# A Fourier mixing block with its feed-forward block: the first batch's first products, and the order of the weight rounding ahead of step 0

## The chip, the core and the metric

The kernel runs on one core of a Trainium2 chip. TensorE (PE) multiplies, VectorE (DVE), ScalarE (ACT) and GpSimd (POOL) do elementwise work, and SyncE (SP) and ACT issue the transfers. The metric is the device time of one execution in microseconds, lower being better. The kernel before takes 1934.93 us, the median of three runs (1934.9 to 1937.18).

## The reference

```
X = np.fft.fft(x, axis=1); X = np.fft.fft(X, axis=2)      # x: 8 x 3008 x 256
x = X.real.reshape(24064, 256)
h = x @ w_in                                              # 256 x 2048
g = h * (1 / (1 + exp(-1.702 * h)))
out = g @ w_out                                           # 2048 x 256
```

For each of the 8 batches a two-dimensional Fourier transform is taken along the sequence (3008 rows) and the model axis (256), its real part goes through a feed-forward block with the quick GELU. The weights arrive as 64-bit floats and are rounded to 32 bits on the core.

## The kernel before

The sequence length is split as 47 x 64. The *first products* (`mix_first` for batch 0, `mix1` for the others) combine the 47 rows that share a residue jj with a cosine or sine table; their result is written to DRAM (`Td`, the *spill*) and read back in another order (`t4`, the *fill*). `rotate` corrects one column, `stage2` multiplies by the 64-point tables and DVE transposes the result into `pq`. The transform along the model axis is not done on the data: it is folded into `w_in` (`fold_w`, chunk by chunk, into `wcs`). After that come 384 *steps*, 8 batches x 3 blocks x 2 halves x 8 pairs of feature blocks. Step t runs `hidden` (four 128x128 products into `pa` and `pb`), `rows` (DVE makes the four arguments of the GELU from `pa`, `pb`, the row `nb` and the per-feature column `af2`), `activate` (the GELU on ACT) and, three steps later, `product` (seven or eight products with `wo` and `wt` into four accumulators).

Every engine works through its instructions in the order in which the code calls them, so the order of the calls is the schedule. Around the change it is this.

- `load_first` (line 225) brings x of batch 0 in sixteen transfers, half of them on SP's queue and half on POOL's: 128 partitions, as two halves of 64, the even and the odd part of the 64 residues; some rows are loaded twice. `tab1` (0.8 MB, first-product tables) comes on ACT's queue.
- `fold_first(g)` (line 232) adds and subtracts x and its mirror for eight groups of four slots: two DVE additions of 128x508 and one POOL copy of 128x8 per group, in the order 0, 7, 1, 6, 2, 5, 3, 4.
- `mix_first(k)` (line 239), four calls, makes 32 products each on 64x64 pieces of the array; four pieces can run beside each other. Between its two phases ACT copies two columns (line 248) as a join. `spill` and `fill(0, 0, 4)` follow.
- A chunk of weights goes through `bounds` (POOL clamps into `m`, line 360; DVE or ACT squares into `g`; ACT makes the low part `r` in two passes), `rounded` (three DVE passes of 128x1024, lines 373 to 376) and `finish` (one or two POOL additions, line 380). There are four chunks of `w_in` ("in") and four of `w_out` ("out"). A chunk of `w_in` then passes `fold_w` (four products of 128x512, line 418, and two ACT copies into `wcs`). `fold_w` ends with a row that ACT doubles and a small transfer that lays it out as four columns of `af2` (line 425).
- Before step 0, chunk in 0 is rounded and folded; in 1 is rounded after `stage2`; out 0, in 2, out 1, in 3, out 2 and out 3 are rounded inside steps 0 to 6 (`ahead`, line 632), one per step, and chunks 1, 2, 3 of `w_in` are folded in steps 1, 3 and 5 (`early`, line 638). Chunk n serves steps 2n and 2n+1 of each group of eight.
- `warm(n)` issues products on a constant tile whose result nobody reads.

Of the kernel before, what the change touches and what calls it, by code (L numbers as in the profile page):

```python
# [36 lines left out]
NM = 48  # L37
# [23 lines left out]
def tables(S, D):  # L61
# [13 lines left out]
    up = np.zeros_like(w1[:, :NJ + 1])  # L75
    up[:, 1:NJ, :, 0], up[:, 1:NJ, :, 1] = cos[:, :NJ:-1], -sin[:, :NJ:-1]
    up[:, e0, :, 1], up[:, o0, :, 1] = cos[:, NJ], sin[:, NJ]
    w0 = np.zeros((2, 64, NJ + 1, NG * NU, 2))
    for half, w in enumerate((w1[:, :NJ + 1], up)):
        w0[half, :32], w0[half, 64 - (NA - 32):] = w[:32], w[32:]  # L80
    sign = np.repeat([1.0, -1.0], 64)

    c, q = np.divmod(np.arange(NJ), 16)
    j, k2 = (4 * (q // 2) + 2 * (q % 2) + c)[:, None], np.arange(NB)[None, :]
    beta = 2.0 * np.pi * ((j * k2) % NB) / NB
    m2 = np.zeros((NU, 2, NJ, 2, NB))
    rot = np.zeros((NU, 2, NJ, NU, 2, NJ))
    ends = np.stack([np.ones(NB), 1.0 - 2.0 * (np.arange(NB) % 2)])
    for i in range(NU):
        m2[i, 0, :, 0], m2[i, 1, :, 0] = np.cos(beta), -np.sin(beta)  # L90
        m2[i, 0, :, 1], m2[i, 1, :, 1] = np.sin(beta), np.cos(beta)
        m2[i, :, 0, 0] = m2[i, :, 0, 1] = ends
        for n in range(NJ):
            rot[i, 0, n, i, 1, n], rot[i, 1, n, i, 0, n] = (1.0, -1.0) if n else (0.0, 0.0)
        rot[i, 0, 0, i, 0, 0] = rot[i, 1, 0, i, 1, 0] = 1.0
# [6 lines left out]
    small = [t.reshape(128, -1) for t in (m2, rot, cd)]  # L102
    pad = 64 - NM
    w1 = np.pad(w1.reshape(NA, -1), ((0, 128 - NA), (0, pad)))
    w0 = np.concatenate([w0.reshape(128, -1), np.zeros((128, pad)), sign[:, None]], 1)
# [4 lines left out]
def kernel(ctx: ExitStack, tc, x, w_in, w_out, tab1, tab2, out):  # L110
# [24 lines left out]
    small = const.tile([128, 2 * NB + 128 + 4 * H], F32, tag="small", name="small")  # L135
    m2 = small[:, 0:2 * NB].rearrange("p (c n) -> p c n", c=2)
    rot = small[:, 2 * NB:2 * NB + 128]
    cd = small[:, 2 * NB + 128:].rearrange("p (i c d) -> p i c d", i=2, c=2)
    wcs = [const.tile([128, DF], F32, tag=f"wcs{i}", name=f"wcs{i}") for i in range(2)]

    wo = const.tile([128, NF // 2, 4, H], F32, tag="wo", name="wo")
    wt = const.tile([128, NF // 2, 4, H], F32, tag="wt", name="wt")
    af2 = const.tile([128, NF], F32, tag="af2", name="af2")
    ones = const.tile([1, 128], F32, tag="ones", name="ones")

# [76 lines left out]

    room = {}

    def load_first(lo, hi):
        for g in range(2):
            for half, eng in enumerate((nc.sync, nc.gpsimd)):
                p = 64 * half + 32 * g
                eng.dma_start(out=xt[p:p + 32, lo:hi, :].rearrange("p j d -> p (j d)"),  # L229
                              in_=view(x, (NB * (NA - 32) * g + NJ * half + lo) * D, [NB * D, 32], [1, (hi - lo) * D]))  # L230

    def fold_first(g):

        t, e = xt[:, 4 * g:4 * g + 4, :], room[g]
# [4 lines left out]
    def mix_first(k):  # L239


        ks = k, 7 - k
        ps = [bank("ps1") for _ in ks]
        for phase in range(2):
            if phase:

                for n in range(2):
                    nc.scalar.copy(af2[:, n:n + 1], ps[n][:, D + n * (H + 1):D + n * (H + 1) + 1])
            for at in range(4)[::-1 if phase else 1]:
                r, even = divmod(at, 2)  # L250
                for half in (phase, 1 - phase):
                    n = half ^ phase
                    for c in range(2):
                        jj = 4 * ks[n] + 2 * r + c
                        c0, c1 = (0, H + 1) if even ^ half ^ phase else (H + 1, D)
                        slot, first = ((NB - jj) % NJ if half else jj), c0 == 0
# [9 lines left out]
    def placed(k):  # L266
        return 2 * k if k < 4 else 16 + 2 * k
# [449 lines left out]
```

## Time and profile before

| | us |
|---|---|
| median of three runs | 1934.93 |
| the profiled execution, its own time | 1932.74 |
| its span on the core | 1930.7 |
| PE busy | 1902.4 (99%) |
| DVE, POOL, ACT busy | 1406.3, 765.0, 673.9 |
| step 0's first product starts | 43.86 |
| first product of step 8 (second half of block 0) starts | 95.92 |

The span is counted from the first to the last instruction of the core; the profiled execution's own time is 2.04 us longer. A line of the timeline gives the start and the length of a run of equal instructions, the engine, the source line, the operation, what it writes and reads, how many there were, and in brackets how long the engine stood idle before it and what ended that. Matmuls of 32-bit floats appear as two records each.

### The profile page before, as it was taken

What the parts mean: (1) busy time and instruction counts of PE and PEld (TensorE: products, weight loads), DVE (VectorE), ACT (ScalarE), POOL (GpSimd) and SP (SyncE); (2) the same over time, 40 slices, a digit from 0 to 9 for tenths busy, and PEclk for the clock granted to TensorE, in tenths of its full rate; (3) what the DMA queues carried; (4) which work ended last, traced back from release to release, by engine and by line L of the source; (5) the groups of instructions that cost most, each with busy time, mean ns of one, the idle gap of its engine ahead of it and who ended that gap; (6) DMA issues with size and microseconds to landing.
All of it is one profiled execution on the core that took longest, in us unless ns stands there. A gap on an engine that the chain in (4) does not pass through costs nothing.

```text
span 1930.7 us, 29514 instructions
## 1 busy us (share of the span) xinstructions
PE 1902.4 (99%) x10822; PEld 1666.2 (86%) x10822; DVE 1406.3 (73%) x2924; ACT 673.9 (35%) x928; POOL 765.0 (40%) x1061
## 2 busy tenths in 40 slices
PE   7899999999999999999999999999999999999998
PEld 4698888988889888888889888898888988889887
DVE  4777777876777767877777677776777777777766
ACT  4633333333333333333333333333333333333332
POOL 3665323542245322552235523364323642223222
PEclk8999999999999999999999999999999999999999
DMA  8720550227203452126322262221820223202201
GB/s 282 178 51 10 110 65 12 51 55 112 17 12 59 67 92 17 25 45 107 51 28 48 40 102 38 18 49 43 121 20 13 18 48 56 17 12 27 17 12 22
DMA packets 145552, 104.54 MB, mean 54 GB/s; under 512 B 105474, under 2 KB 128290, under 8 KB 143712
## 3 DMA queue, kind: packets, MB, share of 16 engines
q1 hardware_dynamic: 142976, 99.07, 30.4%
q0 software_dynamic: 384, 2.10, 0.4%
q8 instruction: 86, 1.41, 0.3%
q10 hardware_dynamic: 2048, 1.48, 0.3%
q14 instruction: 58, 0.48, 0.1%
HBM read 59.36 MB, written 48.01 MB: 56 GB/s over the span
## 4 chain that ended last, share of the span: by engine, by line
PE 96%; DMA 2%; POOL 1%; issue 1%; DVE 0%; ACT 0%; SPq 0%; ACTq 0%; POOLq 0%; DVEq 0%
PE po L515 59%; PE pa L448 17%; PE pb L448 17%; PE ps L210 1%; PE ps L314 1%; DMA xt<-in_x_dram 1%; DMA raw<-in_moe_w_in_dram 1%; DMA Td<-xt 0%; POOL wo L380 0%; PE ps L214 0%; POOL xt L229 0%; PE psw L418 0%; PE ps L259 0%; DVE e L237 0%; POOL wst L380 0%
## 5 line engine op out<-in xcount | busy, mean ns | idle before, releaser
L489 POOL TENSOR_TENSOR s<-h 128x256 f32<-128x256 f32 (+1 forms) x376 | 270.7, 720 | 1091.8 <-ACT h L477 1026.1
L515 PE MATMUL po<-s,wt 128*128 128x256 f32 (+1 forms) x2256 | 599.7, 375 | 0.0
L452 ACT COPY v<-pa 128x512 f32<-128x512 f32 (+1 forms) x384 | 222.2, 579 | 1063.6 <-PE pa L448 1063.6
L462 DVE TENSOR_TENSOR h<-v,pb 128x512 f32<-128x512 f32 (+1 forms) x384 | 259.2, 675 | 405.9 <-PE pb L448 399.5
L515 PEld LDWEIGHTS po<-s,wt 128*128 128x128 f32 x2256 | 428.6, 190 | 48.3
L515 PE MATMUL po<-h,wo 128*128 128x256 f32 (+1 forms) x1632 | 469.7, 375 | 0.1
L477 ACT ACTIVATE h<-h 128x1024 f32<-128x1024 f32 (+1 forms) x384 | 401.0, 1044 | 17.0 <-DVE h L472 14.0
L448 PE MATMUL pa<-pq,wcs 128*128 128x256 f32 (+1 forms) x1536 | 393.9, 379 | 2.9 <-ACT wcs L420 1.6
L448 PE MATMUL pb<-pq,wcs 128*128 128x256 f32 (+1 forms) x1536 | 387.9, 375 | 2.5 <-DVE dif L465 2.3
L515 PEld LDWEIGHTS po<-h,wo 128*128 128x128 f32 x1632 | 310.0, 190 | 36.0 <-issue 0.5
L448 PEld LDWEIGHTS pa<-pq,wcs 128*128 128x128 f32 x1536 | 286.7, 190 | 51.7 <-issue 11.2
L465 DVE SCALAR_TENSOR_TENSOR dif<-nb,af,pb 128x256 f32<-128x256 f32 (+1 forms) x768 | 328.5, 470 | 1.6 <-DMA af<-row 1.6
L448 PEld LDWEIGHTS pb<-pq,wcs 128*128 128x128 f32 x1536 | 291.5, 190 | 36.6 <-DVE dif L465 2.7
L490 POOL TENSOR_TENSOR s<-h 128x256 f32<-128x256 f32 (+1 forms) x376 | 276.7, 736 | 0.0
L472 DVE TENSOR_TENSOR h<-pa,dif 128x512 f32<-128x512 f32 (+1 forms) x448 | 265.5, 605 | 13.2
L515 PE MATMUL po<-h,wt 128*128 128x256 f32 (+1 forms) x752 | 220.3, 375 | 0.0
L515 PE MATMUL po<-s,wo 128*128 128x256 f32 (+1 forms) x752 | 220.3, 375 | 0.0
L493 DVE TENSOR_TENSOR s<-h,s 128x256 f32<-128x256 f32 (+1 forms) x376 | 202.2, 538 | 12.9
L492 DVE TENSOR_TENSOR s<-s,h 128x256 f32<-128x256 f32 (+1 forms) x376 | 178.0, 473 | 4.3 <-POOL s L489 4.3
L515 PEld LDWEIGHTS po<-s,wo 128*128 128x128 f32 x752 | 142.9, 190 | 16.1
L515 PEld LDWEIGHTS po<-h,wt 128*128 128x128 f32 x752 | 142.9, 190 | 16.1
L196 POOL TENSOR_TENSOR xt<-xt 111x510 f32<-111x510 f32 x56 | 74.1, 1323 | 4.4
(67 smaller groups left out, 697.2 us busy)
## 6 DMA issues: line engine op xcount, KB each, us to landing
out_dram<-os SPq DMA_DIRECT2D x284, 64.0 KB
Td<-xt SPq DMA_DIRECT2D x14, 768.0 KB
t<-Td SPq DMA_DIRECT2D x7, 1536.0 KB
xt<-in_x_dram SPq DMA_DIRECT2D x14, 512.0 KB
xt<-Xr SPq DMA_DIRECT2D x14, 512.0 KB
nb<-pq SPq DMA_DIRECT2D x23, 256.0 KB
out_dram<-os SPq DMA_DIRECT2D x96, 56.0 KB
Xr<-in_x_dram SPq DMA_DIRECT2D x7, 752.0 KB
```

What stands on the lines that cost most here:

```text
L196: eng.tensor_tensor(low, low, free(t, up + D - 1, [-D, 2], [-1, D - 1]), op=ALU.add)
L448: nc.tensor.matmul(ps[:, i * 256:i * 256 + n], lhsT=wcs[cs][:, f * 128:(f + 1) * 128], rhs=pq[:, cs, ks], start=True, stop=True)
L452: nc.scalar.copy(two(v[:], n), two(pa[:], n))
L462: nc.vector.tensor_tensor(two(h[:], n), two(v[:], n), two(pb[:], n), op=ALU.add)
L465: nc.vector.scalar_tensor_tensor(dif[:, i * 256:i * 256 + n], nb[:, ks], af2[:, f:f + 1], pb[:, i * 256:i * 256 + n], op0=ALU.mult, op1=AL ...
L472: nc.vector.tensor_tensor(free(h[:], 512 + at + m - 1, [256, 2], [RUN, blocks], [-1, m]), *ins, op=ALU.add)
L477: nc.scalar.activation(g, g, ACTF.Gelu_apprx_sigmoid)
L489: eng.tensor_tensor(s1, a21, a22, op=ALU.add)
L490: eng.tensor_tensor(s3, a11, a21, op=ALU.subtract)
L492: eng.tensor_tensor(s2, s1, a11, op=ALU.subtract)
L493: eng.tensor_tensor(s4, a12, s2, op=ALU.subtract)
L515: nc.tensor.matmul(pot[q][:, i, :n], lhsT=lhs, rhs=rhs, start=(p == 0 and i == 0 and f == 0), stop=(p == NP - 1), skip_group_check=True)
```

## The change

- x of batch 0 is loaded as the 94 half-rows of 32 residues lie in DRAM (96 partitions, neighbouring partitions being the two halves of one row), in six transfers, all on SP's queue: four of 384 KB and two of 768 KB. POOL issues none.
- The two halves now lie on alternate partitions. `matrices()` makes, from the table, four sets of full-width matrices `pair` (own and other half, zero where the partition belongs to the other, with the sign for the difference part): eight multiplications of 128x720, three on ACT, three on POOL, two on DVE. `specials()` adds four of 128x48 on POOL. The rooms for the folded data are cleared on partitions 64 to 127 (four memsets of 64x1024 each on DVE and POOL). `wo` and `wt` are one tile now, and the tables lie in it.
- `mix_first(i)`, eight calls, makes eight products each on the whole 128x128 array, 127 or 129 columns wide, for two jj at a time, into one bank, and one ACT copy brings it out. No join of columns.
- Spills go out as jj 1 to 8, 9 to 12, 13 to 15 and 0, each on SP and ACT; the load of chunk out 0 is issued after the first of them, those of in 2 and out 1 right after `fill(0, 0, 4)`; the rest of the fill is issued in step 1.
- The second table `m2f` serves batch 0, as its jj lie in another order. The transposes after `stage2` run cs by cs.
- Chunks in 0, in 1 and out 0 are rounded before step 0, all on the same engines as before, and chunks 0 and 1 of `w_in` are folded before it; `warm` is called for 3 products in place of 5. Five chunks remain for the steps, from step 0, and chunks 2 and 3 are folded in steps 2 and 4.
- `fold_w` makes the four columns of `af2` with four products of one column (`psf`) and an ACT copy; the row, its doubling and its transfer go. The tile `m` has two buffers.

```diff
-    up = np.zeros_like(w1[:, :NJ + 1])
-    up[:, 1:NJ, :, 0], up[:, 1:NJ, :, 1] = cos[:, :NJ:-1], -sin[:, :NJ:-1]
-    up[:, e0, :, 1], up[:, o0, :, 1] = cos[:, NJ], sin[:, NJ]
-    w0 = np.zeros((2, 64, NJ + 1, NG * NU, 2))
-    for half, w in enumerate((w1[:, :NJ + 1], up)):
-        w0[half, :32], w0[half, 64 - (NA - 32):] = w[:32], w[32:]
-    sign = np.repeat([1.0, -1.0], 64)
+    w0 = np.zeros((128, NJ + 1, NG * NU, 2))
+    low, high = w0[0:2 * NA:2], w0[1:2 * NA:2]
+    low[:] = w1[:, :NJ + 1]
+    high[:, 1:NJ, :, 0], high[:, 1:NJ, :, 1] = cos[:, NJ + 1:], -sin[:, NJ + 1:]
+    high[:, e0, :, 1], high[:, o0, :, 1] = cos[:, NJ], sin[:, NJ]
+    odd = np.arange(128)[:, None] % 2
+    kinds = np.concatenate([1.0 - odd, odd, -1.0 * odd, 1.0 - 2.0 * odd], 1)
...
-    wo = const.tile([128, NF // 2, 4, H], F32, tag="wo", name="wo")
-    wt = const.tile([128, NF // 2, 4, H], F32, tag="wt", name="wt")
+    wot = const.tile([128, 2, NF // 2, 4, H], F32, tag="wo", name="wo")
+    wo, wt = wot[:, 0], wot[:, 1]
     af2 = const.tile([128, NF], F32, tag="af2", name="af2")
     ones = const.tile([1, 128], F32, tag="ones", name="ones")
+    twos = const.tile([1, 1], F32, tag="twos", name="twos")
...
     def load_first(lo, hi):
-        for g in range(2):
-            for half, eng in enumerate((nc.sync, nc.gpsimd)):
-                p = 64 * half + 32 * g
-                eng.dma_start(out=xt[p:p + 32, lo:hi, :].rearrange("p j d -> p (j d)"),
-                              in_=view(x, (NB * (NA - 32) * g + NJ * half + lo) * D, [NB * D, 32], [1, (hi - lo) * D]))
+        nc.sync.dma_start(out=xt[0:96, lo:hi, :].rearrange("p j d -> p (j d)"),
+                          in_=view(x, lo * D, [NJ * D, 96], [1, (hi - lo) * D]))
+    def matrices():
+        kinds = [w0[:, n0 + i:n0 + i + 1] for i in range(3)]
+        tasks = iter((nc.scalar, nc.gpsimd, nc.vector) * 4)
+        for s0, own, other in ((1, 0, 1), (17, 1, 0)):
+            src = w0[:, s0 * NM:(s0 + 15) * NM].rearrange("p (s m) -> p s m", m=NM)
+            for even in (1, 0):
+                for c, kind in enumerate((own, other)):
+                    out, by = pair[:, even, s0:s0 + 15, c * NM:(c + 1) * NM], kinds[kind if even or not kind else 2]
+                    eng = next(tasks)
+                    if eng is nc.scalar:
+                        eng.activation(out, src, ACTF.Copy, scale=by)
+                    else:
+                        eng.tensor_scalar(out, src, scalar1=by, scalar2=None, op0=ALU.mult)
+    def specials():
+        for even, at in ((1, 0), (0, NJ)):
+            nc.gpsimd.tensor_copy(pair[:, even, 0, 0:NM], w0[:, at * NM:(at + 1) * NM])
+        w16 = w0[:, 16 * NM:17 * NM]
+        nc.gpsimd.tensor_copy(pair[:, 1, 16, NM:], w16)
+        nc.gpsimd.tensor_scalar(pair[:, 0, 16, NM:], w16, scalar1=w0[:, n0 + 3:n0 + 4], scalar2=None, op0=ALU.mult)
     def fold_first(g):
-        t, e = xt[:, 4 * g:4 * g + 4, :], room[g]
+        t, e = xt[0:2 * NA, 4 * g:4 * g + 4, :], room[g][0:2 * NA]
         nc.gpsimd.tensor_copy(free(e, 0, [D, 4], [H, 2]), free(t, 0, [D, 4], [H, 2]))
         for at, op in ((1, ALU.add), (H + 1, ALU.subtract)):
             nc.vector.tensor_tensor(e[:, :, at:at + H - 1], t[:, :, 1:H], free(t, D - 1, [D, 4], [-1, H - 1]), op=op)
-    def mix_first(k):
-        ks = k, 7 - k
-        ps = [bank("ps1") for _ in ks]
-        for phase in range(2):
-            if phase:
-                for n in range(2):
-                    nc.scalar.copy(af2[:, n:n + 1], ps[n][:, D + n * (H + 1):D + n * (H + 1) + 1])
-            for at in range(4)[::-1 if phase else 1]:
-                r, even = divmod(at, 2)
-                for half in (phase, 1 - phase):
-                    n = half ^ phase
-                    for c in range(2):
-                        jj = 4 * ks[n] + 2 * r + c
-                        c0, c1 = (0, H + 1) if even ^ half ^ phase else (H + 1, D)
-                        slot, first = ((NB - jj) % NJ if half else jj), c0 == 0
-                        w, m = (w0o, jj) if jj and not first else (w0, jj or ENDS[1 - first])
-                        rows_ = slice(64 * half, 64 * half + 64)
-                        nc.tensor.matmul(ps[n][64 * c:64 * c + 64, r * D + c0:r * D + c1], lhsT=mat(w, m, rows_),
-                                         rhs=room[slot // 4][rows_, slot % 4, c0:c1], start=(phase == 0 and at == 0),
-                                         stop=(phase == 1), skip_group_check=True)
-        for n in range(2):
-            to = placed(ks[n])
-            nc.scalar.copy(xt[:, to:to + 2, :].rearrange("p j d -> p (j d)"), ps[n][:])
-    def placed(k):
-        return 2 * k if k < 4 else 16 + 2 * k
+    def mix_first(i):
+        ps, ns = bank("ps1"), (2 * i + 1, 2 * i + 2) if i < 7 else (0, 15)
+        for at, n in enumerate(ns):
+            for even in range(2):
+                c0, c1 = (0, H + 1) if even else (H + 1, D)
+                o = ps[:, at * D + c0:at * D + c1]
+                for k, slot in enumerate((n, NJ - n if n else 16)):
+                    rhs = room[slot // 4][:, slot % 4, c0:c1]
+                    w = free(pair[:, even, slot], 0, [1, 128])
+                    nc.tensor.matmul(o, lhsT=w, rhs=rhs, start=(k == 0), stop=(k == 1))
+        to = free(xt[:], ns[0] * D, [(ns[1] - ns[0]) * D, 2], [1, D])
+        nc.scalar.copy(to, free(ps[:], 0, [D, 2], [1, D]))
+    def spill_first(lo, hi):
+        for c, eng in enumerate((nc.sync, nc.scalar)):
+            eng.dma_start(out=view(Td[0], (16 * c + lo) * D, [NJ * D, NM], [1, (hi - lo) * D]),
+                          in_=xt[NM * c:NM * c + NM, lo:hi, :].rearrange("p q d -> p (q d)"))
...
+        m = m2 if b else m2f
...
-        for u in range(NU):
-            for cs in range(2):
+        for cs in range(2):
+            for u in range(NU):
...
-        m = cv.tile([128, 1024], F32, tag="m", name="m")
+        m = cv.tile([128, 1024], F32, tag="m", bufs=2, name="m")
         r = cv.tile([128, 1024], U32, tag="r", bufs=2, name="r")
+        nc.gpsimd.tensor_scalar(m[:], hi, scalar1=TOP, scalar2=-TOP, op0=ALU.min, op1=ALU.max)
         if first:
             nc.vector.tensor_tensor(g[:], hi, hi, op=ALU.mult)
         else:
             nc.scalar.activation(g[:], hi, ACTF.Square)
-        nc.gpsimd.tensor_scalar(m[:], hi, scalar1=TOP, scalar2=-TOP, op0=ALU.min, op1=ALU.max)
...
-        row = cv.tile([1, 512], F32, tag="e", name="row")
-        nc.scalar.activation(row[:], ps[0:1, :], ACTF.Copy, scale=2.0)
-        nc.scalar.dma_start(out=af2[:, 4 * n:4 * n + 4], in_=row[:])
+        ps = bank("psf")
+        for f in range(4 * n, 4 * n + 4):
+            nc.tensor.matmul(ps[:, f:f + 1], lhsT=wcs[1][0:1, f * 128:f * 128 + 128], rhs=twos[:], start=True, stop=True)
+        nc.scalar.copy(af2[:, 4 * n:4 * n + 4], ps[:, 4 * n:4 * n + 4])
...
-    w0 = wt[:].rearrange("p a q n -> p (a q n)")[:, 0:n0 + 1]
-    w0o = wt[:].rearrange("p a q n -> p (a q n)")[:, 2048:2048 + n0]
+    flat = wot[:].rearrange("p w a q n -> p (w a q n)")
+    pair = flat[:, 0:2 * NJ * 2 * NM].rearrange("p (e s m) -> p e s m", e=2, s=NJ)
+    w0 = flat[:, 6176:6176 + n0 + 4]
...
+    for i, e in enumerate(rooms):
+        (nc.vector, nc.gpsimd)[i % 2].memset(e[64:128], 0.0)
+    nc.vector.memset(flat[:, 6144:6176], 0.0)
+    nc.vector.memset(free(pair[:, 0, 0], 0, [2 * NJ * NM, 2], [16 * 2 * NM, 2], [1, 2 * NM]), 0.0)
     nc.vector.memset(ones[:], 1.0)
-    nc.scalar.dma_start(out=w0, in_=tab1[:, 0:n0 + 1])
-    for lo in (0, 24, 8, 16):
-        load_first(lo, lo + 8)
+    nc.vector.memset(twos[:], 2.0)
+    nc.scalar.dma_start(out=w0, in_=tab1[:, 0:n0 + 4])
+    for part in ((0, 4), (28, 32), (4, 8), (24, 28), (8, 16), (16, 24)):
+        load_first(*part)
     load_in(0, nc.sync)
     nc.sync.dma_start(out=small[:], in_=tab2)
     load_in(1, nc.sync)
     warm(7)
     nc.scalar.copy(af2[0:1, 0:1], ones[0:1, 0:1])
-    nc.scalar.activation(w0o, w0[:, 0:n0], ACTF.Copy, scale=w0[:, n0:n0 + 1])
-    for k, need in enumerate(((0, 7, 1), (6, 2), (5, 3), (4,))):
+    matrices()
+    for i, need in enumerate(((0, 7), (1,), (6,), (2,), (5,), (3,), (4,), ())):
         for g in need:
             fold_first(g)
-        mix_first(k)
-        if k:
-            for m in ((0, NM),) if k < 3 else ((0, 16), (16, NM)):
-                spill(0, ((0, 2), (2, 1), (3, 1))[k - 1], (nc.sync, nc.scalar if k > 1 else nc.sync), *m)
-                if k == 3 and m[0] == 0:
-                    fill(0, 0, 4)
-    load_out(0, nc.sync)
-    bounds(("in", 0), True)
+        mix_first(i)
+        if i == 2:
+            specials()
+        if i == 3:
+            spill_first(1, 9)
+            load_out(0, nc.sync)
+        if i == 4:
+            bounds(("in", 0), True)
+        if i == 5:
+            spill_first(9, 13)
+    spill_first(13, 16)
+    spill_first(0, 1)
+    fill(0, 0, 4)
+    load_in(2, nc.sync)
+    load_out(1, nc.sync)
     round_in(0)
     finish_in(0)
-    warm(5)
-    bounds(("in", 1))
-    fold_w(0)
-    fill(0, 4, NG)
-    load_out(1, nc.sync)
-    rotate(0, 0, 4, nc.scalar.copy)
-    stage2(0, 0)
+    bounds(("in", 1), True)
     round_in(1)
     finish_in(1)
+    fold_w(0)
+    warm(3)
     bounds(("out", 0))
-    load_in(2, nc.sync)
+    round_out(0)
+    finish_out(0)
+    rotate(0, 0, 4)
+    stage2(0, 0)
+    fold_w(1)
+    bounds(("in", 2))
     extra, early = {}, {}
@@ -629,13 +649,14 @@
     n = len(steps)
-    ahead = [("out", 0), ("in", 2), ("out", 1), ("in", 3), ("out", 2), ("out", 3)]
+    ahead = [("in", 2), ("out", 1), ("in", 3), ("out", 2), ("out", 3)]
     for t, (kind, c) in enumerate(ahead):
         at(t, round_out if kind == "out" else round_in, c)
         if t + 1 < len(ahead):
             at(t, bounds, ahead[t + 1])
         at(t + 1, finish_out if kind == "out" else finish_in, c)
-    early[1], early[3], early[5] = 1, 2, 3
+    early[2], early[4] = 2, 3
+    at(1, fill, 0, 4, NG)
     for t, load, c in ((0, load_in, 3), (1, load_out, 2), (2, load_out, 3)):
         at(t, load, c, nc.sync)
```

In `combine`, which runs once in eight steps, `u4` shares the buffer of `u2`; its operations and their order stay.

## The prediction

> **What bounds the kernel now.** I read the chain that ended last first, as the page gives PE as busy for 99% of the span: the question is where the other 28 us are.
>
> ```profile
> 4.87 16.95 DMA xt<-in_x_dram
> ...
> 30.59 2.58 DMA Td<-xt
> ...
> 39.18 12.18 DMA raw<-in_moe_w_in_dram
> ...
> 69.83 3.48 POOL wo L380 x2
> ...
> 77.62 1.13 PE pb L448 x4
> 78.75 3.45 PE po L515 x16
> 82.21 3.43 PE psw L418 x8
> 85.64 0.86 PE pa L448 x4
> ```
>
> From 77.62 on the chain is PE alone, to the end of the span: every microsecond won or lost before that moves the end by as much, and of the change only the order of the transposes and the shared buffer of `u2` come later, DVE work beside a full PE. Before it the chain is x, spill and fill, the load of chunk in 2, then the rounding on POOL, ACT and DVE. So I price the change at one mark: the moment when PE has done steps 0 to 5 of `hidden`, 0 to 2 of `product` and all four `fold_w`. Before, that is 85.64.
>
> Next the timeline, for what DVE and POOL need for a group of x and for a chunk:
>
> ```profile
> 14.71 2.48 DVE L237 TENSOR_TENSOR first<-xt 128x508 f32<-128x508 f32 x4 [2.48 <-DMA xt<-in_x_dram]
> ...
> 27.77 1.23 DVE L373 SCALAR_TENSOR_TENSOR m<-g,m 128x1024 f32<-128x1024 f32 x1
> 29.04 0.69 DVE L375 TENSOR_SCALAR a<-m 128x1024 uint32<-128x1024 uint32 x1
> 29.76 1.23 DVE L376 SCALAR_TENSOR_TENSOR a<-m,a 128x1024 uint32<-128x1024 uint32 x1
> ...
> 33.81 2.37 POOL L380 TENSOR_TENSOR wst<-a,r 128x1024 uint32<-128x1024 uint32 x1 [8.42 <-ACT r L363]
> ...
> 36.14 1.12 POOL L360 TENSOR_SCALAR m<-raw 128x1024 f32<-128x1024 f32 x1
> ```
>
> A group costs DVE 1.24; a chunk costs DVE 3.22 (27.77 to 30.99), then POOL 2.37, and POOL's clamp of the next chunk 1.12. Last, the windows, for the clock and the transfers (columns: PE, PEld, DVE, ACT, POOL busy, clock, DMA share, GB/s):
>
> ```profile
> 8.00:13.00 5.00, 1.86 (x7) 0.48 (x5) 1.29 (x2) 0.42 (x1) 0.70 (x1) 0.82 1.04 285
> 13.00:19.00 6.00, 2.26 (x32) 1.76 (x32) 4.19 (x7) 0.32 (x2) 2.40 (x4) 0.50 1.00 272
> 19.00:26.00 7.00, 6.43 (x144) 5.46 (x146) 4.87 (x8) 2.71 (x8) 3.55 (x5) 0.83 1.01 350
> ```
>
> The DMA engines are full, at 272 to 285 GB/s while both queues bring x and at 350 once mostly weights come. PE idled at 9 to 12 and 13 to 16, and its clock is half for all of 13 to 19.
>
> **What the skill says.** The Trainium skill, TensorE: Matmul & The Clock Gate, Part 1 (The HAM clock gate): the clock halves after a window of some 3.4 us with too little work and returns after a busy one. The trace agrees: 0.50 after those idle stretches, 1.00 from 26 on, although PE pauses there too, never for most of a window. Same page, Part 3 (Packing small matmuls): matmuls on different parts of the array run beside each other; agrees, 32 products of 64x64 pieces took 1.83 of PE (24.44 0.71 and 25.44 1.12 in the chain). SBUF — State Buffer, Who interferes with whom: a POOL operation waits out a DVE operation with two inputs from SBUF, or the reverse; this trace shows it at most as single lengthenings (clamp 1.41 for 1.12).
>
> **The change part by part.** Times are in this execution's span.
>
> *Loads.* x falls from 4.19 MB (sixteen of 256 KB) to 3.15 MB. The table lands as before, about 6.7 (ACT's first use was at 6.79). By 6 some 1.2 MB had moved (windows: 160 GB/s to 5, then 307); 2.8 MB of x and 1.05 MB of in 0 remain. POOL's queue brings nothing now, and streams on one queue alone ran at about 390 GB/s in this trace (4 KB packets of 160 ns on 16 engines, 21 to 26 us). Bounds: 280, as x came before, to 395. I take 390: in 0 is there at 6 + 3.85/0.39 + 0.4 = 16.3; at 280 it is 20.1.
>
> The load of out 0 now stands in SP's queue ahead of the later spills: 1.05 MB, 2.7, issued near 18.5 and gone before the next spill at 23. In 2 and out 1 follow the fill, at about 31, and land by 41, before their use at 43 (before, in 2 landed at 51.4, the 12.18 of the chain: that stall goes). The rest of the fill moves to step 1 and is read in step 4, 25 later. All three free.
>
> *Ahead of the first product.* Memsets: the trace has 128x512 at 0.48 and 128x128 at 0.17, so about 0.9 each, four per engine beside each other from 1.4, done by 6: free, the table comes later. Eight products of 128x720: DVE's nearest row is 128x1024 at 0.69, so 0.6 each (bounds 0.5 and 1.2), ACT's 128x1600 at 1.63 gives 0.8, POOL's 128x1024 at 1.12 gives 0.8 to 1.5. DVE is through at 7.9, ACT and POOL by 9.2. POOL's `specials` wait for the first mix and lie in POOL's queue ahead of the copies of groups 2 and 5; four at 0.3 to 0.7 still end before DVE gets there: free.
>
> *DVE's queue.* Six groups at 1.27 from 7.9: 15.5. Then the square of in 0, which waits for in 0 and has groups 3 and 4 queued behind it: 16.3 to 17.5; two groups: 20.0; the rounding of in 0: 23.2.
>
> *The first mix.* 64 products of 127 or 129 columns at four cycles a column are 0.213 each at full clock (the 128x512 of `psw` takes 0.86, a quarter of it is the same), 1.71 per call, 13.7 in all, where four calls with array pieces took 7.3. It starts at about 10.5 and follows DVE; PE ends near 25, copies and spill follow, 2.6 to land, 4.2 for the fill (chain: 33.79 4.22): t4 at about 33. Nobody asks for it before 33.6. Twice the PE work, on nobody's path.
>
> *Three chunks in a row.* POOL finishes in 0: 23.2 + 2.37; clamps in 1: 26.8; DVE 3.22: 30.0; POOL finishes in 1: 32.4; clamps out 0: 33.6; DVE: 36.8. Behind that in DVE's queue stands the copy of `rotate`, for which the second half of `stage2` waits: 37.0. This is the new path. `fold_w(0)` (25.6 to 29), `psf` and `warm(3)` lie beside it, after which PE stands idle to 37.0.
>
> *Before step 0.* stage2's second half 0.9: 37.9; `fold_w(1)` 3.44: 41.3; the copy of wcs1 0.86; four `psf`. No row has these: 0.9, by the price in the Trainium skill, TensorE: Matmul & The Clock Gate, LDWEIGHTS (loading weights takes columns/1.2 ns, here 107 ns, and each product comes twice; the trace's own weight loads, hidden behind matmuls, read 190), an estimate; upper bound 2.8 by `rotate`'s own product (0.41 + 0.28). Step 0 at 43.1, before 43.86.
>
> *Steps 0 to 5.* ACT makes g and r of in 2 first (3.26 by its timeline), then `v` 0.59; `rows(0)` 2.25 ends at 49.5 (before: 51.01; the 1.59 wait for the `af2` transfer is gone). From there DVE has a chunk and a `rows`, 5.47 per step. In 2 rounded at 52.7, folded from 55.1 to 58.5; DVE's `rows(2)` ends at 60.4, whose bank `psf` takes: 61.3. hidden 3 and 4 (1.72 each), products 0 and 1 (3.41 each): 71.5; `fold_w(3)` 75.0; copy and `psf` 76.7; `rotate` 0.3; hidden 5, product 2: 82.2. That is 3.4 less than 85.64.
>
> *What comes on top.* Some dozen handovers between engines at 0.05: 0.6. And the clock: PE is idle from about 34.5 to 37.0, with a moment of `stage2`, and again 53.9 to 55.1; a window[...] costs up to 1.7 of `fold_w`'s 3.44. Before, no window of this stretch was lost. Bounds none and two, 0 to 3.4; I take one and a half, 2.5, as the idle stretches are about a window long. Sum: 82.2 + 0.6 + 2.5 = 85.3, 0.3 less than before.
>
> **Rivals.** A difference of under 0.2%, 3.9 us, can't be told from no change.
> 1. *The chain of chunks replaces the load chain, and the two come out even* (forecast). For: every row above is from the trace. The profiled execution would be 1932.74 - 0.3, the median 1934.6. Own range 1931.3 to 1938.6.
> 2. *Slower: the square of in 0 at the head of DVE's queue.* If x and in 0 come at 272 GB/s, as in 13 to 19, in 0 lands at 20.5, and the square holds groups 3 and 4, the mix and all rounding behind it, 4.2 longer: 1938.8; with dear `psf` 1940. It counts from any landing later than 15.5, and decides from about 20.5. For it: x had this rate. Against: it had it with POOL's queue beside it.
> 3. *Faster: no window lost, `psf` at half its price.* 3.4 - 0.6 + about 1.3: 4.1 less, 1930.8. Against: the idle stretches of PE are in the order of the calls.
> 4. *The wide first mix becomes the path*, as it doubles PE's work. It would have to end 3.5 later than I have it; at half clock for one window it is 1.7. This leaves rival 1's time.
>
> **How the numbers follow.** Rivals 1 and 4: 0.67. Rival 2: 0.19. Rival 3: 0.14. Predicted 1934.6. The range for 8 in 10 runs from 1931.0 to 1939.2: it takes in both bounds of the clock and most of the x rate's. These are also the chances of same, slower and faster.
>
> **What would show it.** In the profile after: in 0 landed (POOL's clamp, DVE's square) at about 16; the square of in 0 with little idle before it; `rotate`'s copy right after DVE's third chunk, near 37; step 0 near 43 to 45; a PE clock below full between 35 and 42. Wrong would be a square that waits until 20, a fill that lands after DVE's third chunk, or PE not closed up by the mark.

## The result, and the profile after

The changed kernel takes 1938.36 us, the median of four runs (1937.43 to 1939.32), beside 1934.91 of the kernel before in the same session (1934.33 to 1937.18). The ratio is 1.0016, its 95% interval 0.9998 to 1.0033. The profiled execution took 1937.43 with a span of 1935.6 (before 1932.74 and 1930.7). The forecast of 1934.6 stood for no difference that can be told; the range held the time, but the small step went up and not down, and the mark shows where it arose: it is at 90.79, before 85.64, and was predicted at 85.3. (The traced execution of before is 2.2 below its median, that of the changed kernel 0.9, so the marks lie further apart than the medians.)

The longer pieces of the chain of waits of the changed kernel, up to the mark (start, length, what):

```profile
0.73 7.05 DMA wo<-in_tab_dram
8.03 2.01 issue
10.69 1.98 issue
12.67 3.00 POOL wo L244
15.72 12.28 PE ps L270 x78
28.61 1.11 ACT r L367
29.74 1.06 ACT r L368
30.88 2.35 POOL wst L385
33.23 1.11 POOL m L361
...
62.36 5.41 PE psw L423 x8
...
87.34 3.45 PE po L521 x16
```

The load of in 2, 12.18 of the chain before, is gone. In its place stand the table, POOL's multiplications (L244; twice 2 us of "issue", in which POOL waits for nothing that the profile shows), the first mix (L270), ACT's low part of in 0 behind it, and three chunks in a row (30.88 to 44.3). At 62.36 a `fold_w` takes 5.41 in place of 3.45.

The timeline has what the chain only touches:

```profile
7.96 7.71 POOL L244 TENSOR_SCALAR wo<-wo 128x720 f32<-128x720 f32 x3 [3.62 <-DMA wo<-in_tab_dram]
...
9.55 4.25 DVE L258 TENSOR_TENSOR first<-xt 94x508 f32<-94x508 f32 x6
...
20.92 1.23 DVE L364 TENSOR_TENSOR g<-raw 128x1024 f32<-128x1024 f32 x1 [1.19 <-DMA raw<-in_moe_w_in_dram]
...
30.88 2.35 POOL L385 TENSOR_TENSOR wst<-a,r 128x1024 uint32<-128x1024 uint32 x1 [5.95 <-ACT r L368]
```

POOL's three multiplications take 2.1, 2.7 and 3.0 (7.71 in all) while DVE works beside them. The square of in 0 waits for its chunk until 20.9. POOL's finish of in 0 stands idle for 5.95 and is released by ACT's low part, not by DVE.

The windows answer to those of before (PE, PEld, DVE, ACT, POOL busy, clock, DMA share, GB/s):

```profile
8.00:13.00 5.00, 2.02 (x6) 0.68 (x4) 5.00 (x7) 2.27 (x3) 5.00 (x3) 0.90 1.06 256
13.00:19.00 6.00, 3.28 (x13) 3.08 (x14) 4.36 (x7) 0.00 (x0) 5.30 (x11) 0.50 0.97 267
19.00:26.00 7.00, 7.00 (x51) 7.00 (x50) 5.81 (x8) 1.76 (x3) 3.96 (x3) 0.77 0.67 270
```

x alone on one queue runs at 256 GB/s, slower than on two queues before, at a full DMA share; and the mix runs at half clock to 22.2. Against the prediction's own steps:

| | predicted | measured |
|---|---|---|
| in 0 landed | 16.3 | 20.9 |
| last multiplication done | 9.2 | 15.67 |
| first mix ends | 25 | 33.3 |
| POOL's finish of in 0 starts | 23.2 | 30.88 |
| `rotate`'s copy | 37.0 | 44.32 |
| step 0's first product | 43.1 | 50.49 |
| `rows(0)` ends | 49.5 | 56.64 |
| mark | 85.3 | 90.79 |

The error is there in full at POOL's finish of in 0 (7.7), stays at 7 to 7.5 through the three chunks up to `rows(0)`, and shrinks to 5.5 after that. So the experiments ask what makes in 0 late, and then whether the order behind it is worth its price.

### The profile page after: what moved, and what is told of

Its sections match the earlier page's. It is cut to its first block, busy times and chain, and to the rows that moved or that the text cites. A ratio compares the mean times of both kernels' runs of the same rounds, so it can differ in the third digit from the quotient of the medians.

```text
span 1935.6 us, 29331 instructions
## 1 busy us (share of the span) xinstructions
PE 1914.0 (99%) x10722; PEld 1680.3 (87%) x10722; DVE 1417.6 (73%) x2935; ACT 670.4 (35%) x920; POOL 771.3 (40%) x1064
## 4 chain that ended last, share of the span: by engine, by line
PE 97%; DVE 1%; POOL 1%; issue 0%; ACT 0%; DMA 0%; POOLq 0%
PE po L521 59%; PE pa L454 17%; PE pb L454 17%; PE ps L213 1%; PE ps L319 1%; PE psw L423 1%; PE ps L270 1%; DMA wo<-in_tab_dram 0%; PE ps L217 0%; POOL wst L385 0%; POOL wo L244 0%; DVE m L378 0%; PE psf L430 0%; DVE a L381 0%; POOL m L361 0%
## 5 line engine op out<-in xcount | busy, mean ns | idle before, releaser
L521 PE MATMUL po<-s,wo 128*128 128x256 f32 (+1 forms) x3008 | 759.0, 375 | 0.0
L521 PE MATMUL po<-h,wo 128*128 128x256 f32 (+1 forms) x2384 | 689.9, 375 | 0.0
L521 PEld LDWEIGHTS po<-s,wo 128*128 128x128 f32 x3008 | 572.1, 190 | 63.9
L521 PEld LDWEIGHTS po<-h,wo 128*128 128x128 f32 x2384 | 453.5, 190 | 51.2
L555 DVE TENSOR_TENSOR c<-u,po 128x256 f32<-128x256 f32 (+1 forms) x188 | 69.4, 410 | 1.6
L325 DVE STREAM_TRANSPOSE pq<-ps 128x256 f32<-128x256 f32 x96 | 34.6, 418 | 44.6 <-PE ps L319 44.6
L555 DVE TENSOR_TENSOR u<-u,po 128x256 f32<-128x256 f32 (+1 forms) x141 | 57.8, 410 | 9.5 <-ACT u L526 4.6
L538 DVE STREAM_TRANSPOSE os<-c 128x512 f32<-128x512 f32 x94 | 61.1, 687 | 0.1
```

The costliest lines, as they stand in the source:

```text
L521: nc.tensor.matmul(pot[q][:, i, :n], lhsT=lhs, rhs=rhs, start=(p == 0 and i == 0 and f == 0), stop=(p == NP - 1), skip_group_check=True)
L555: nc.vector.tensor_tensor(out_, i0, i1, op=how)
```

## The experiments

All of them, with the mark (for b4, c1, c3 and d1, where `fold_w(3)` comes behind product 2, the end of its `psf`):

| run | step 0 | mark | time | ratio to before, interval |
|---|---|---|---|---|
| before | 43.86 | 85.64 | 1934.91 | |
| changed | 50.49 | 90.79 | 1938.36 | 1.0016 (0.9998 to 1.0033) |
| a1 multiplications off POOL | 49.07 | 89.33 | 1937.60 | 1.0015 (1.0008 to 1.0021) |
| a2 low part of in 0 early | 49.92 | 91.88 | 1938.71 | 1.0020 (1.0013 to 1.0027) |
| a3 both | 47.75 | 88.76 | 1936.37 | 1.0009 (1.0000 to 1.0018) |
| a4 rows of x close together | 52.12 | 93.19 | 1938.32 | 1.0017 (1.0010 to 1.0024) |
| b1 x in three forms | 49.30 | 90.44 | 1937.06, one run | |
| b2 warm products | 50.22 | 90.48 | 1937.49 | 1.0012 (1.0005 to 1.0019) |
| b3 = a3, low part of in 2 late | 50.13 | 90.44 | 1936.15 | 1.0008 (0.9999 to 1.0016) |
| b4 = b3 and five edits | 45.79 | 83.64 | 1930.47 | 0.9980 (0.9973 to 0.9988) |
| c1 = b4, x on 128 partitions | 48.16 | 86.00 | 1935.36 | 1.0004 (0.9995 to 1.0012) |
| c2 = a3, x on 128 partitions | 49.73 | 90.00 | 1936.40 | 1.0010 (1.0003 to 1.0017) |
| c3 = changed, old chunk order | 44.76 | 87.42 | 1934.11 | 0.9999 (0.9990 to 1.0007) |
| d1 = c1, small operations on ACT | 43.40 | 81.24 | 1928.39 | 0.9964 (0.9950 to 0.9978) |

Ratios are each to the kernel before, run in the same session. The mark is read from one execution, and half-clock windows that fall differently move it by 1 to 2.

### a1: the multiplications off POOL

```diff
-        tasks = iter((nc.scalar, nc.gpsimd, nc.vector) * 4)
+        tasks = iter((nc.scalar, nc.vector) * 4)
```

> The changed kernel with POOL's three multiplications of 128x720 given to ACT and DVE (four each, in turn). Mark: the moment when PE has done hidden 0 to 5, product 0 to 2 and the four fold_w; 90.79 in the changed kernel, 85.64 before. Theory 1 (POOL's multiplications, 2.6 us each in place of 0.8, hold the first mix and that alone is the loss): the mix runs from about 11.5 instead of 15.7 and the mark returns to about 86. Theory 2 (the late chunk in 0 with DVE's square ahead of groups 3 and 4 is the loss): mix starts earlier too, but POOL's finish of in 0 and the mark stay (30.9 and 90.8). Theory 3 (both in a row: ACT's low part of in 0 stands behind the copy of mix 4 and hides DVE's delay): the low part comes at about 23 instead of 28.5, POOL's finish of in 0 then starts when DVE's rounding ends, at 28.6, 2.3 earlier, and the mark is about 88.5.

Theory 3: POOL's finish of in 0 starts at 28.59, when DVE is done, as expected, and the mark is at 89.33 (88.5 expected). Eight multiplications on ACT and DVE took 0.81 and 0.89 each and were done at 11.3. POOL's share costs 1.5 at the mark; the loss is not this alone. What is left ahead of POOL's finish is in the chain, the late chunk in 0 and the square and rounding behind it:

```profile
4.05 16.70 DMA raw<-in_moe_w_in_dram
20.76 1.23 DVE g L364
...
28.59 3.19 POOL wst L385
```

That is the wait of rival 2. In the changed kernel it ran beside the late mix and was hidden by it: DVE's rounding of in 0 ended there at 28.6 too, ACT's low part at 30.8.

### a2: the low part of in 0 off the mix

```diff
-        if i == 4:
-            bounds(("in", 0), True)
+        if i == 2:
+            low0 = low_part(("in", 0))
+        if i == 6:
+            bounds(("in", 0), True, low0)
```

> The changed kernel with the bounds of in 0 taken apart: ACT's low part after the copy of mix 2, DVE's square and POOL's clamp after group 4. Theory 1 (the mix is the path only through ACT's queue): POOL's finish of in 0 starts when DVE's rounding ends, at about 26.7 (square 22.3 to 23.5, rounding 3.2) instead of 30.9; the three chunks are done 4.2 earlier (rotate's copy free to go at about 40). If nothing else is late, the mark falls from 90.8 to about 86.6. Theory 2 (the late mix also delays spill and fill, and the fill is next): the fill still lands at about 43, step 0 starts only 0.5 earlier, and the mark is about 90.

(`low_part` is ACT's two passes, taken out of `bounds`.) Theory 2. POOL's finish of in 0 came at 27.7, 3.2 earlier, and nothing followed from it: step 0 is 0.57 earlier, and the mark is later only because another half-clock window fell on hidden 5 and product 2. Its chain, last spill and fill:

```profile
33.30 5.21 DMA Td<-xt
...
38.85 4.21 DMA t<-Td
...
43.20 0.35 PE psr L305 x2
```

The late mix has two ways to step 0, one through ACT to the chunks and one through spill and fill, and they are about equally late. On rival 2 this says little: the square of in 0 stood behind groups 3 and 4 here, but the mix, held up by POOL's multiplications, was late whatever the square did.

### a3: both

> Both edits together: no multiplication on POOL, low part of in 0 after mix 2, square and clamp after group 4. If the late mix and the order around in 0 together are the loss: last mix ends near 26 instead of 33.3, fill lands near 36, POOL's finish of in 0 starts at about 26.7, rotate's copy comes at about 40.3 instead of 44.3, and the mark at about 86.7, near the 85.64 of the kernel before; time about 4 us under the changed kernel's. If the loss lies after step 0 (clock, order on ACT), the mark stays above 89.

Step 0 is 2.7 earlier and the mark 2.0, half of what was expected for the mark. The chain starts with x, 14.40 of transfers until 17.8, so x is what is late ahead of step 0. The mix ended at 29.5 and not at 26, and the square of in 0 took 2.10 in place of 1.23 beside POOL's clamp, which took 2.18 in place of 1.12: a collision that was not priced.

### a4 and b1: why x comes at 250 GB/s

a4:

```diff
-                          in_=view(x, lo * D, [NJ * D, 96], [1, (hi - lo) * D]))
+                          in_=view(x, lo * D, [4 * D, 96], [1, (hi - lo) * D]))
```

> The changed kernel, but the 96 partitions of x are read 4 KB apart in DRAM instead of 32 KB apart (other rows of x: batch 0's output is another one; sizes, packets and all other work are the same). Theory A (the distance of the rows in DRAM sets the 250 GB/s): x comes at about 400 GB/s, in 0 lands at about 16.5 instead of 20.9. Theory B (the queue, the writing side or the start of the kernel sets it): 250 GB/s again, in 0 at 20.9. For the mark: with theory A and a loss from the late x alone, about 86; with the mix behind POOL's multiplications as the later of the two, it stays at about 90 even if x comes faster, because ACT's low part still waits for the copy of mix 4.

242 to 245 GB/s from 6 to 14, in 0 at 22.1: theory B, the distance of the rows is not it. b1:

```diff
+        n = 128 if lo in (4, 28) else 96
+        src = view(x, lo * D, [NJ * D, n], [1, (hi - lo) * D])
+        if lo in (8, 16):
+            src = w_in[0:96, lo * 64:lo * 64 + 1024].bitcast(F32)
```

> The changed kernel with x's six transfers in three forms, all else the same: slots 0 to 3 and 24 to 27 on 96 partitions as before; slots 28 to 31 and 4 to 7 on 128 partitions (32 more rows, which nobody reads); slots 8 to 23 on 96 partitions of 4 KB each, read from w_in in place of x (the output of batch 0 is another one). In the changed kernel a packet of 4 KB of x took 265 ns, one of the weights, right behind x on the same queue, 160 ns. Theory A (96 partitions are the cause): the 128-partition transfers run at about 400 GB/s, those from w_in at about 250. Theory B (where x lies in DRAM is the cause): the transfers from w_in run at about 400, the 128-partition ones at about 250. Theory C (the time since the start, or the tile xt): all at about 250.

Its windows, first over the two transfers of 128 partitions, then over those of 96 from `w_in`:

```profile
7.00:8.00 1.00, 1.00 (x4) 0.41 (x3) 0.54 (x1) 0.54 (x1) 0.38 (x1) 1.00 1.03 410
...
11.00:12.00 1.00, 0.09 (x1) 0.00 (x0) 1.00 (x2) 0.00 (x0) 1.00 (x1) 0.86 1.02 258
12.00:13.00 1.00, 0.00 (x0) 0.00 (x0) 1.00 (x3) 0.00 (x0) 1.00 (x2) 0.50 1.02 246
```

Theory A: the same x, the same queue and tile, 410 GB/s on 128 partitions; the weights, which come at 410 on 128 partitions, fall to about 250 on 96. A third more bytes take less time: 4.19 MB at 410 GB/s are 10.2, 3.15 MB at 250 are 12.6 (an estimate from these rates; in d1, below, in 0 lands behind the larger x at 18.0 and not at 20.9). The Trainium skill says where to look (SBUF — State Buffer, Door 1: The DMA port swizzle): partitions 0 to 63 reach only half of the 16 ports, 64 to 127 the other half. By that map 96 partitions load the first half as fully as 128 do, which would give three quarters of 410, 308 as an estimate from that page; the trace has 250, so the direction agrees and the size is not explained.

### b2: the clock at fold_w(2)

```diff
+        if t == 2:
+            keep(4)
         if t in early:
             fold_w(early[t])
```

> The changed kernel with four products of 128x512 on a constant tile ahead of fold_w(2) in step 2, in an accumulator that nobody uses yet; they fill PE's idle time from about 58 to 62. Theory 1 (the half clock in fold_w(2), 5.41 in place of 3.45, is part of the loss): fold_w(2) takes 3.45 again and the mark falls by 2.0, from 90.8 to 88.8. Theory 2 (DVE is the bound there: psf of chunk 2 and hidden 3 wait for the bank of rows(2), which DVE leaves at 68.2): fold_w(2) takes 3.45, but psf still starts at about 68.3, and the mark falls by no more than 0.3.

```profile
62.06 3.71 PE psw L429 x8
...
66.43 1.05 PE psf L436 x8
67.48 1.06 PE pa L460 x4
...
83.51 1.67 PE pa L460 x4
85.18 1.71 PE pb L460 x4
```

In the chain, `fold_w(2)` is at full clock, and `psf` and hidden 3 start 2.0 earlier than in the changed kernel: theory 1 is right at that place, and `psf` does not wait for `rows(2)`, which DVE ends at 68.0. But 1.7 of it is lost again at 83.5, where hidden 5 runs at half clock after the pause of `fold_w(3)`'s copy and `psf`. The mark gains 0.3. That the warm products moved the loss there is not shown: a2, without them, lost as much at hidden 5 and product 2, with `fold_w(2)` at half clock as well. And the trace is of one execution, of 1937.09; six of the twenty took 1934.96 to 1935.35, the others 1936.0 to 1938.73.

### c3: the old chunk order

The first products, x, table and `psf` stay as changed; rounding, loads and folds go in the order of the kernel before (its core):

```diff
     round_in(0)
     finish_in(0)
-    bounds(("in", 1), True)
-    round_in(1)
-    finish_in(1)
+    warm(5)
+    bounds(("in", 1))
     fold_w(0)
-    warm(3)
-    bounds(("out", 0))
-    round_out(0)
-    finish_out(0)
-    rotate(0, 0, 4)
+    fill(0, 4, NG)
+    load_out(1, nc.sync)
+    rotate(0, 0, 4, nc.scalar.copy)
     stage2(0, 0)
-    fold_w(1)
+    round_in(1)
+    finish_in(1)
```

> The changed kernel with the old order of the chunks: only in 0 rounded ahead of step 0, in 1 right after stage2, the other six in steps 0 to 5, fold_w(1), (2), (3) in steps 1, 3 and 5, the rest of the fill, out 1 and in 2 loaded as before the change; first products, x, table and psf as changed. Theory 1 (the new chunk order gains: it takes away the wait for in 2 and the short steps, and the loss is all in the first products): the mark is at or above the 90.8 of the changed kernel. Theory 2 (rounding three chunks ahead is itself the loss, since rotate's copy and step 0 wait for the third): step 0 follows the fill, at about 45.5 instead of 50.5; from step 0 to the mark it took 41.8 in the kernel before, so the mark is at about 87.3 and the time about 3 below the changed kernel's, near that of the kernel before.

Theory 2: step 0 at 44.76, mark 87.42, and a time that can't be told from that of the kernel before. The end of `fold_w(3)`'s four products, which is the mark of the kernel before, is at 85.70 here and 85.64 there. The slow first products, less what `psf` gains, cost nothing that the time shows. The old wait is back in the chain, and it is cheaper than what replaced it:

```profile
39.79 11.66 DMA raw<-in_moe_w_in_dram
```

So the new chunk order costs 3.4 at the mark when in 0 is late. Which part of it does is argued, not shown, as c3 puts several things back at once. In the changed kernel `rotate`'s copy stands behind DVE's rounding of out 0, a chunk that POOL finishes at 44.6 to 47.1 and that product 0 first needs at 71.40; but it comes only 0.5 after `rotate`'s own product there (2.1 in a1, 1.3 in a3). And `fold_w(1)` with its `psf`, 3.7 and 1.05, stands ahead of step 0 and in c3 behind it.

### b3 and b4: the order around step 0

b3 is a3 with `add_low`, ACT's two passes for in 2, called at the start of step 0's extras, behind `v` and `nb`.

> The kernel a3 (no multiplication on POOL, bounds of in 0 taken apart) with ACT's two passes for the low part of in 2 after v and nb of step 0 instead of before. Theory 1 (DVE has no idle time from rows(0) to rows(2), so v of step 0 sets the mark): v at 49.8 instead of 51.1, rows(2) 1.3 earlier, mark 1.3 earlier than in a3: 88.77 to 87.5. Theory 2 (POOL's finish of in 2 and fold_w(2) set it): finish waits for the later low part or for DVE, whichever is later; DVE's rounding also moves 1.3, so fold_w(2) moves 1.3 too, and with it the half-clock window may fall elsewhere: mark between 86 and 88.5. If neither v nor the rounding of in 2 is on the path: no change, 88.8.

From hidden 0 to the end of `rows(0)` it took 5.30 in place of 6.14: `nb` is late next, so 0.84 and not 1.3. In this execution step 0 is 2.4 later than in a3, 1.0 of it ahead of `stage2`'s second half and 1.4 in a half-clock window there and in `fold_w(1)`, so the mark rose; the time is a3's within its interval. Inconclusive for the whole. b4:

```diff
+    load_out(0, nc.sync)
     warm(7)
...
+    rotate(0, 0, 4)
+    stage2(0, 0)
     bounds(("out", 0))
     round_out(0)
     finish_out(0)
-    rotate(0, 0, 4)
-    stage2(0, 0)
...
-        ps = bank("psf")
+        ps = first_ps
...
-    early[2], early[4] = 2, 3
+    whens = (0, 2, 3, 4, 5)
+    early[2], early[5] = 2, 3
...
+        if t == 2:
+            keep(4)
```

> The kernel b3 with five more edits: the load of out 0 issued right after that of in 1; rotate and stage2 called ahead of the rounding of out 0; psf in the bank of the first psw, without a bank of its own; out 1 and the chunks behind it rounded one step later (out 1 in step 2, in 3 in step 3, fold_w(3) in step 5); four warm products ahead of fold_w(2). If DVE's queue between step 0 and hidden 3 is what holds the mark: rotate's copy follows the fill instead of the third chunk, 1.3 earlier; psf no longer waits for rows(2), 1.0; DVE has one rounding (about 4.2 with its collisions) less ahead of rows(2), of which some 2 to 3 reach PE; mark near 82 to 83.5, below the 85.64 of the kernel before, and a time of 1931 to 1933, 2 to 4 below it. If something else holds it (the fill, transfers behind the later loads), the mark stays above 85 and the time is that of the kernel before or more.

Close to what was expected: mark 83.64, time 1930.47, under both kernels. `rotate`'s copy is at 39.45, right behind its product (a3: 41.59). Five edits were made at once; what each is worth was not tried.

### c1, c2 and d1: faster x, and POOL's small operations

```diff
-        nc.sync.dma_start(out=xt[0:96, lo:hi, :].rearrange("p j d -> p (j d)"),
-                          in_=view(x, lo * D, [NJ * D, 96], [1, (hi - lo) * D]))
+        nc.sync.dma_start(out=xt[:, lo:hi, :].rearrange("p j d -> p (j d)"),
+                          in_=view(x, lo * D, [NJ * D, 128], [1, (hi - lo) * D]))
...
-    warm(7)
+    warm(10)
```

c1 is b4 with both edits, c2 is a3 with the first.

> The kernel b4 with x of batch 0 loaded on 128 partitions instead of 96 (32 rows more in each transfer, which nobody reads; 4.19 MB in place of 3.15) and ten warm products at the start instead of seven. If the 96 partitions cost what b1 shows (250 against 400 GB/s): x is there at about 16 and in 0 at about 18.5 instead of 20.5, although a third more is moved; with PE kept busy to 12.1 the first mix runs at full clock and ends 1.5 to 2 earlier (28.7 instead of 30.3), the fill lands at about 37, and the mark falls from 83.6 to about 82: time 1929, 1.5 below b4. If DVE's folds or PE's mix bind there rather than x, only the clock counts: 0 to 1 less. If the added bytes cost more than the rate gives: in 0 later than 20.5 and a time above 1930.5.

> The kernel a3 (no multiplication on POOL, bounds of in 0 taken apart) with x of batch 0 on 128 partitions, nothing else. Theory 1 (the rest of the error ahead of step 0 is x's rate): in 0 lands at about 18 instead of 20.5; DVE is through the folds at 21.0 instead of 21.7, POOL's clamp no longer collides with the square, rounding of in 0 ends at about 25.4 instead of 27.2, and rotate's copy and step 0 are 1.8 earlier (step 0 at 46 instead of 47.75, mark 87 instead of 88.8). Theory 2 (DVE's own work, four multiplications and eight groups, binds): in 0 earlier, step 0 within 0.5 of 47.75. Theory 3 (more bytes, later): step 0 after 48.

Both missed, and this was the most useful miss. x came at 407 to 441 GB/s, and yet step 0 was 2.4 later than in b4 and 2.0 later than in a3. The timeline of c1 says why:

```profile
10.27 3.66 DVE L258 TENSOR_TENSOR first<-xt 94x508 f32<-94x508 f32 x6
...
10.46 10.64 POOL L256 COPY e<-xt 94x8 f32<-94x8 f32 x1 [1.01 <-DMA xt<-in_x_dram]
...
13.85 6.05 DVE L258 TENSOR_TENSOR e<-xt 94x508 f32<-94x508 f32 x10
...
19.83 1.21 DVE L375 TENSOR_TENSOR g<-raw 128x1024 f32<-128x1024 f32 x1
```

A copy of 94x8, which takes 0.20 at other times, stood for 10.64, until DVE had gone through sixteen folds and the square. PE, whose next product needs it, was busy for 0.00 from 18 to 21. With x slow DVE pauses for x, and POOL gets its turn: the same copy stood for 5.34 in b4 and 5.39 in a3, from which c1 and c2 were made, in both until DVE paused. So the slow x had hidden half of this.

It need not come to this. In the kernel before, beside the four folds in a row from 14.71 that the prediction shows, three copies of 128x8 were through after one fold each, 0.66 to 0.72; the first two:

```profile
14.74 1.32 POOL L235 COPY first<-xt 128x8 f32<-128x8 f32 x2 [3.05 <-DMA xt<-in_x_dram]
```

In the changed kernel four took 0.65 to 1.25 beside such folds. What decides whether POOL gets in between two DVE operations is not shown.

d1 is c1 with these operations on ACT (all eight copies called ahead of the first mix):

```diff
-        nc.gpsimd.tensor_copy(free(e, 0, [D, 4], [H, 2]), free(t, 0, [D, 4], [H, 2]))
+        nc.scalar.copy(free(e, 0, [D, 4], [H, 2]), free(t, 0, [D, 4], [H, 2]))
```

> The kernel c1 with POOL's small operations of the first products on ACT: the eight copies of 94x8 that close the folds (all called ahead of the first mix) and the four of specials (after mix 4). In c1 the copy for group 6 stood on POOL from 10.46 to 21.1, as long as DVE worked without a pause, and PE had nothing to do from 17.5 to 21.1. Theory 1 (POOL's operation can't begin while DVE's run back to back, however short it is): on ACT the copies take 0.2 each as soon as x has landed, PE follows DVE, the mix ends at 26.5 to 28 instead of 32.7, the fill lands at about 36 instead of 41.4, step 0 starts at 42.5 to 44 instead of 48.2, the mark is at 80 to 82 instead of 86.0, and the time 4 to 6 below c1's 1935.4, so under b4's 1930.5. Theory 2 (the copies waited for something else, the landing of x or PE): they are as late on ACT, PE stands as long, and step 0 and the time stay within 1 of c1's.

```profile
12.99 0.21 ACT L256 COPY e<-xt 94x8 f32<-94x8 f32 x1 [2.23 <-DMA xt<-in_x_dram]
13.90 6.06 DVE L262 TENSOR_TENSOR e<-xt 94x508 f32<-94x508 f32 x10
15.54 0.42 ACT L256 COPY e<-xt 94x8 f32<-94x8 f32 x3 [2.33 <-DMA xt<-in_x_dram]
...
18.18 3.90 POOL L376 TENSOR_SCALAR m<-raw 128x1024 f32<-128x1024 f32 x1 [13.83 <-DMA raw<-in_moe_w_in_dram]
```

Theory 1: the copies take 0.2 as x lands, the mix ends at 27.2, step 0 starts at 43.40 and the mark is at 81.24. The time is 1928.39, ratio 0.9964 (0.9950 to 0.9978): the fastest of all. It is 7.0 below c1's by the medians, more than expected, and 4.5 by the traced executions (1928.29 and 1932.82): three of c1's thirteen executions, the traced one among them, took about 1932.8, the others 1934.5 to 1936.1, and no trace shows where those lost. What still reads SBUF on POOL is held up here too: the clamp of in 0, 1.1 elsewhere, stands from 18.18 to 22.1; DVE's square ends at 21.1.

## Why the prediction was right in its range and wrong in its steps

- *Forecast and range.* Right for the time, 3.8 above the value and 0.8 inside the upper end. This is in part luck: POOL's finish of in 0 was 7.7 late, two late paths lay side by side so that only the later one counted, and 2.2 was made up by the mark. Right that the chain of chunks replaces the load chain: the wait for in 2 is gone from the chain, and c3 brings it back.
- *"ACT and POOL by 9.2"* (multiplications): here the sum first went wrong. The table came at 7.8, not 6.7. Then POOL's three, priced at 0.8 each by a row that stood alone, with a bound of 1.5, took 2.1, 2.7 and 3.0 and ended at 15.67; they were costed at nothing. a1 prices them at 1.5 of the mark. How much of their length is DVE's doing is not shown: the first ran for 1.6 of its 2.1 beside DVE's own multiplications, before the folds began, and no run has one alone.
- *The copies of the folds*: I did not price them at all. In the changed kernel the mix never waits for them; with x fast they and `specials` cost 4.8 at the mark (c1 against d1). The page of the Trainium skill cited in the prediction (SBUF — State Buffer, Summary: rules for kernel authors) says that of a DVE operation with two SBUF inputs and a POOL operation that reads SBUF, the second to issue "fully blocks" until the first finishes. The trace of before agrees, one fold for each copy, and I took that as the size of the effect; the 10.64 of c1, through seventeen operations, is more than the page says.
- *"I take 390"* (x): measured 250, below both bounds. The rate came from transfers on 128 partitions, the new ones are on 96 (b1). So the wait of rival 2 did come: the square stood until 20.9, and DVE's rounding of in 0 ended at 28.6, 5.4 later than predicted. It was the second of two late paths, behind the mix (30.8), and the first once the multiplications were gone (a1). Its 1938.8 lies near the measured time, but in the changed kernel's chain stands the other path. x at 410 gained nothing in c2, because the copy then stood for 10.6; no run has x slow and the copies on ACT, so what x's rate alone is worth stays open.
- *The first mix, "on nobody's path"*: wrong; rival 4 happened. It was priced for one window at half clock; the mix started 5.2 later than I had it, ran at half clock from 15.7 to 22.2 and ended 8.3 later. It was left out that ACT's low part of in 0 stands behind the copy of its fifth call. "Twice the PE work" was misread as well: the two rows behind "32 products took 1.83" hold 44 records, which are 22 products. From 24 to 31, 124 records took 4.56, so the four old calls come to about 9.4 (an estimate), against the 13.7 taken for the new ones. No sum used it.
- *Three chunks in a row*: 13.4 from POOL's finish of in 0 to `rotate`'s copy, predicted 13.8. Right in size; that step 0 need not come behind the third was in the order of the calls and was not asked.
- *Before step 0*: 6.17, predicted 6.1, `psf` 1.05 for 0.9. Right.
- *Steps 0 to 5*: 34.15 from the end of `rows(0)`, predicted 35.8 with clock and handovers. The lost window is at `fold_w(2)`, 2.0, predicted 2.5 in all. Wrong in one thing: `psf` does not wait for the bank of `rows(2)` (b2).

How much of the changed kernel's loss comes from the late in 0 and how much from the order is not separated: a3 takes 2.0 off the mark, c3 takes 3.4, and they act on the same wait.

## What to carry to other kernels

When work is moved to POOL beside a DVE that will run without a pause, take the end of DVE's run as the upper bound of its price and not its own length, however small it is: the same small copy took 0.2, 0.7 or 10.6 here, and on ACT 0.2. A stall that you remove may have been the pause in which another engine got its turn, so ask who used it. And before a chunk of work is pulled ahead of a start, ask when it is first needed: here `rotate`'s copy, and so step 0, stood behind the third chunk for a product that came more than 20 us later.

## What the runs showed of the hardware

- A POOL copy of 94x8 stood for 10.64 through seventeen DVE operations in a row, each with two inputs from SBUF (c1, c2 the same), for 5.08 to 5.39 in a1, a3 and b4, each time to the end of DVE's run, and for 3.66 in b3, where it ended while DVE went on. In the changed kernel such copies were through in 0.65 to 1.25 beside DVE's folds, and its multiplications of 128x720 got through at 2.1 to 3.0. What decides stays open.
- A DVE square beside a POOL clamp took 2.10 for 1.23, the clamp 2.18 for 1.12 (a3).
- Transfers to 96 partitions ran at about 250 GB/s with all DMA engines busy, to 128 partitions at about 410, from x and from the weights alike (b1).
- From `fold_w(1)` to the mark, which place loses a clock window differs between nearly equal orders: `fold_w(2)` alone in the changed kernel (5.41 for 3.45), `fold_w(2)` and the products from 85.7 on in a2, `fold_w(1)` and hidden 5 in b2. And PE need not have stood idle throughout: in b2 it was busy for 2.73 of the 3.40 from 80.1 to 83.5, 1.05 of them products of one column, and the clock was half of full from 83.6 to 87.0.
